# New durations for a planner's idle work and first loads, in the opening of a fused attention and expert kernel

## Chip, cores and metric

The kernel runs on one core of one Trainium2 chip. The metric is the device time in microseconds (us) of one execution; the median of eight runs before the change is 1723.44 us (1723.06 to 1723.79). Engines are named as in the profile: PE multiplies matrices, DVE, ACT and POOL work on tiles, SP issues most loads and stores.

## What is computed

Linear attention, normalised, is followed by a weighted sum over four two-layer experts. All of it is in fp32.

```python
# attention: 8 batches, 8 heads, 576 positions, head dimension 64
kv  = np.einsum('bhsd,bhse->bhde', k, v)
out = np.einsum('bhsd,bhde->bhse', q, kv)
rms = np.sqrt(np.mean(out * out, axis=-1, keepdims=True) + 1e-06)
x   = (out / rms * g_norm)            # then (B,H,S,D) -> (B*S, H*D): 4608 rows of 512
# experts: E = 4, D = 512, F = 1024
p = domain_probs / (domain_probs.sum(-1, keepdims=True) + 1e-09)
for e in range(E):
    h = np.maximum(x @ w1[e], 0.0)
    out += p[:, e:e + 1] * (h @ w2[e])
```

## The kernel before, in words

**Stages.** The 4608 rows form nine chunks of 512: one for each of the eight batches (its first 512 positions) and a ninth of the eight remainders of 64 positions. A stage is one chunk with one expert, so there are 36. Each stage has a product up (x by w1, then relu) and a product down (hidden by w2). The very first product up is plain (`up_plain`, L999: 16 groups of two 128x512 products). All others use recursive forms with seven products in place of eight, one or two levels deep (`up`, L912; `down`, L1126; `down_deep`, L1201), whose operand sums are adds on DVE or POOL (L360). Attention of batch c+1 is computed inside stage c.

**Attention of a batch** runs per pair of heads: q is turned by PE (L651) and copied by ACT (L656); k by v is summed on PE (L665) and copied (L678); the attention product follows (L691) into the PSUM banks db and u in batch 0, db or ab later; ACT squares (L564), DVE reduces (L571), POOL takes the power -1/2 (L578, L582), DVE multiplies (L591), PE turns the result (L709), and ACT copies it scaled by the gain (L717). The 64 remaining positions go the same way through L735, L753 and L769. In batch 0 this is done pair by pair, in the others two pairs at a time.

**Who decides the order.** Nothing is ordered by hand. Every operation is given to a planner (`Plan.add`) with a key, a cost in us for each engine that could run it, the buffers it touches and, for loads, a size. At build time `Plan.layout` plays all engines forward: at each moment an engine that is free takes, among operations whose inputs and buffers are ready by the planner's clock, the one with the earliest due time (PE and SP: the first in key order that is ready). An add that either DVE or POOL may do goes to whichever takes it first. Tile slots are given out in the same pass. What comes out is one fixed list for each engine; on the chip every engine works through its list in that order and waits on semaphores.

**Loads in the planner.** A load costs SP 0.55 us; its end is taken from a bus that starts at a fixed time and moves 215 KB a us (L169), with eight loads in flight at most (LANES, L171). The size that a load is given (`kb`) is used for that alone, not for the transfer itself. In the opening SP loads q, k and v of the four pairs of batch 0, then the four quarters of w1 of expert 0, then q, k and v of batch 1.

**Idle work.** While PE is in the opening (its next operation has a key under 0) and nothing is ready for it, the planner inserts idle operations (L204 to L217): two transposes of the identity (L1353) into a bank of ab or db that nobody uses. Each is planned at 0.23 us. They are part of PE's list for good: PE executes them whether or not the next operation could already start.

The lines that set this before the change:

```python
105        bus, port = 3.0, 0.0
169                        bus = max(bus, t + 1.5) + op.kb / 215.0
170                        op.end = bus + 0.5
204                if eng == "PE" and busy[eng] <= t and 1.6 <= t and front < idle_until:
209                        op = Op(front, {"PE": 0.23}, None, (), (), 0, False)
```

Of the kernel before, what the change touches and what calls it, by code (L numbers as in the profile page):

```python
# [16 lines left out]
class Buf:  # L17


    def __init__(self, kind, name, ap=None):  # L20
        self.kind, self.name, self.ap = kind, name, ap
        self.writers, self.readers, self.left, self.slot = [], [], 0, None
# [12 lines left out]
class Plan:  # L35
# [13 lines left out]

    SPARE = {"big": 6, "small": 3}  # L50
    STEP, LATE = 44.0, 20.0

    def __init__(self):
        self.ops = []
# [26 lines left out]
    def layout(self, slots, later, idle, idle_banks, idle_until):  # L81
# [20 lines left out]
                cross = self.SAME if op.cost.keys() == d.cost.keys() else self.CROSS  # L102
                d.due = min(d.due, op.due - cross - min(d.cost.values()))
        busy = {e: 0.0 for e in todo}
        bus, port = 3.0, 0.0
        lanes = [0.0] * self.LANES
        t = 0.0
        wake = [0.0, 1.6]
# [24 lines left out]
        while left:  # L133
            moved = False
            while todo["PE"] and todo["PE"][0].start is not None:
                todo["PE"].pop(0)
            front = todo["PE"][0].key if todo["PE"] else 1e9
            for eng in todo:
                if busy[eng] > t:
                    continue  # L140
                pending = todo[eng]
                while pending and pending[0].start is not None:
                    pending.pop(0)
                if not pending:
                    continue
                reach = pending[0].key + self.REACH[eng]
                best = None
                for op in pending:
                    if op.key > reach:
                        break  # L150
                    if op.start is not None:
                        continue
                    if best is not None and op.due >= best.due:
                        continue
                    when = ready(op, eng)
                    if when is None:
                        continue
                    if when > t:
                        heapq.heappush(wake, when)
                        continue  # L160
                    best = op
                    if eng in ("PE", "SP"):
                        break
                if best is not None:
                    op = best
                    op.start, op.eng = t, eng
                    if eng == "SP":
                        busy[eng] = t + op.cost[eng]
                        bus = max(bus, t + 1.5) + op.kb / 215.0  # L169
                        op.end = bus + 0.5  # L170
                        lanes = lanes[1:] + [op.end]  # L171
                    else:
                        op.end = busy[eng] = t + op.cost[eng]
                        if op.kb:
                            op.end += 9.0 if op.kb == 512 else 5.5
                    if op.port:
                        port = op.end
                        heapq.heappush(wake, port)
                    for b in op.outs:
                        if b.kind is not None and b.slot is None:  # L180
                            free[b.kind].sort()
                            b.slot = free[b.kind].pop(0)[1]
                            b.ap = slots[b.kind][b.slot]
                    for b in op.bufs:
                        b.left -= 1
                        if b.left == 0 and b.kind is not None:
                            end = max(o.end for o in [op] + b.readers + b.writers) + self.CROSS
                            free[b.kind].append((end, b.slot))
                            live[b.kind] -= 1
                            ended[b.kind] = max(end, ended.get(b.kind, 0.0))  # L190
                            for rule in [r for r in later if not any(live.get(k) for k in r[0])]:
                                later.remove(rule)
                                end = max(ended[k] for k in rule[0])
                                for ap in rule[2]:
                                    free.setdefault(rule[1], []).append((end, len(slots[rule[1]])))
                                    slots[rule[1]].append(ap)
                                heapq.heappush(wake, end)
                    heapq.heappush(wake, busy[eng])
                    heapq.heappush(wake, op.end + self.SAME)
                    heapq.heappush(wake, op.end + self.CROSS)  # L200
                    order.append(op)
                    left -= 1
                    moved = True
                if eng == "PE" and busy[eng] <= t and 1.6 <= t and front < idle_until:  # L204
                    kind, spare = next((
                        (k, f) for k in idle_banks for f in free[k] if f[0] <= t
                    ), (None, None))
                    if spare is not None:
                        op = Op(front, {"PE": 0.23}, None, (), (), 0, False)
                        op.start, op.eng, op.end = t, eng, t + 0.23  # L210
                        op.fn = lambda eng, bank=slots[kind][spare[1]]: idle(bank)
                        busy[eng] = op.end
                        free[kind].remove(spare)
                        free[kind].append((op.end, spare[1]))
                        heapq.heappush(wake, op.end)
                        order.append(op)
                        moved = True  # L217
            if moved:
                continue
            while wake and wake[0] <= t:  # L220
                heapq.heappop(wake)
            assert wake, ("no operation can start", t, left, {
                e: (todo[e][0].key, todo[e][0].fn) for e in todo if todo[e]
            }, {k: len(v) for k, v in free.items()})
            t = heapq.heappop(wake)
# [5 lines left out]
def kernel(  # L231
# [41 lines left out]
    NT = 512  # L273
    NR = NT // P
# [5 lines left out]
    KR = 6  # L280
# [83 lines left out]
    def load(key, buf, dst, src, kb, reads=(), also=()):  # L364
        plan.add(
            key, SPC, lambda eng: nc.sync.dma_start(out=dst(), in_=src), reads=reads,
            parts=[buf] + list(also), kb=kb,
        )
# [40 lines left out]
    def w1_src(e, dh, uh):  # L409
        rows = moe_w1[e][dh * 2 * P:(dh + 1) * 2 * P, uh * HF:(uh + 1) * HF]  # L410
        return rows.rearrange("(kt p) f -> p kt f", p=P)
# [19 lines left out]
    def weights_1(e, key, step, need):  # L431

        f = {n: Buf("big", f"w1_{e}_{n}") for n in (1, 2, 21, 4, 5, 6, 7, 3)}
        corner = {}
        w1corner[e] = {}
        for i, (n, dh, uh) in enumerate(((1, 0, 0), (2, 1, 0), (21, 0, 1), (4, 1, 1))):
            corner[n] = Buf(None, f"w1c_{e}_{n}")
            w1corner[e][uh, dh] = f[n], corner[n]
            load(
                key + i * step, f[n],  # L440
                lambda n=n: f[n].ap[:].rearrange("p (k u) -> p k u", k=2),
                w1_src(e, dh, uh), 512, also=[corner[n]],
            )

        def form(k_, o, a, b, op):
# [155 lines left out]
    def attention(b, key, span, rem):  # L601
# [9 lines left out]
        def load_pair(hp):  # L611
            hs = slice(2 * hp, 2 * hp + 2)
            n = f"{b}_{hp}"
            kind = "kv" if b or hp < 2 else "big"
            kt, vt, qt = Buf(kind, f"k{n}"), Buf(kind, f"v{n}"), Buf("small", f"q{n}")
            want = at(hp) - 0.25 if b else key - 1 + 0.1 * hp
            for r in range(2):
                load(
                    want, qt,
                    lambda qt=qt, r=r: qt.ap[:].rearrange(  # L620
                        "p (r h d) -> p r h d", h=2, d=D)[:, :, r, :],
                    q[b, 2 * hp + r, 0:NT, :].rearrange("(p r) d -> p r d", r=NR), 128,
                )
            for t, src in ((kt, k), (vt, v)):
                load(
                    want, t,
                    lambda t=t: t.ap[0:KP, 0:2 * KR * D].rearrange("p (h x) -> p h x", h=2),
                    src[b, hs].rearrange("h (p j) d -> p h (j d)", j=KR), 288,
                )
            return kt, vt, qt  # L630

# [4 lines left out]
        for g, pairs in enumerate(groups):  # L636
            n = f"{b}_{g}"
# [85 lines left out]
        n = f"{b}_r"  # L723
# [584 lines left out]
    plan.add(-2.85, {"SP": 1.1}, load_gains, writes=[gains], kb=1)  # L1308
    attention(0, -2.0, 1.3, 0.1)
    sums_1 = weights_1(0, -2.5, 0.02, 0.3)  # L1310
    up_plain(0, 0, 0, 0.0, 1.0)
    sums_1()
# [44 lines left out]
    with tc.manual_schedule(engines={ENG.PE, ENG.DVE, ENG.Activation, ENG.Pool, ENG.SP}):  # L1357
# [4 lines left out]
        for op in order:  # L1362
            if op.seed:
                bank, n = op.marks
# [39 lines left out]
```

## Time and profile before

| | |
|---|---|
| median of 8 runs | 1723.44 us (1723.06 to 1723.79) |
| the profiled execution | 1723.65 us, of which the span in the trace is 1721.9 us |
| instructions in the trace | 39248 |
| idle transposes in PE's built list | 114 |
| DMA moved | 230.42 MB, mean 134 GB/s |

How to read it: the span is the time from the first to the last recorded instruction, and all times in the trace count from its start. A timeline line gives start, length, engine, line, operation, output and inputs, shapes, and a count where equal instructions were merged; in brackets stands the idle time before it and what ended it. In fp32 a product is two matmul records in the trace, a transpose one. A matmul's recorded length includes its passage through the array, so the distance between the starts of two groups, and not the length, is what a group costs when PE is full. A line of waits gives who waited for whom, the total in us, how often, and the longest. A line of DMA issues ends with the median us from issue to landing.

### The profile page before, as it was taken

The numbers are of one execution on the slowest core, as the hardware profiler recorded it, in microseconds if no ns is written. First come the engines' busy times: TensorE is split into PE (matmuls) and PEld (weight loads), VectorE is DVE, ScalarE is ACT, GpSimd is POOL, SyncE is SP. The second block draws the span as 40 slices with busy tenths as digits, with TensorE's granted clock in tenths as the row PEclk, the third lists the DMA queues.
The fourth block names the chain that finished last, engine by engine and source line by source line (L and its number), as shares of the span: only waits on it lengthen the run. The fifth ranks groups of instructions, "written<-read, shape, count | busy, mean of one in ns | idle before, by whom it ended". The sixth has DMA issues, their size and how long they took to land.

```text
span 1721.9 us, 39248 instructions
## 1 busy us (share of the span) xinstructions
PE 1712.6 (99%) x15586; PEld 1653.8 (96%) x15586; DVE 1234.7 (72%) x2034; ACT 973.9 (57%) x2378; POOL 677.0 (39%) x613
## 2 busy tenths in 40 slices
PE   9999999999999999999999999999999999999998
PEld 7699999999999999999999999999999999999998
DVE  4755655565777777777778787777788787777774
ACT  3354544454455665565666566566666666656562
POOL 2421322133435443433355554433355554433331
PEclk9999999999999999999999999999999999999999
DMA  9756434633456354444478444444478444444442
GB/s 235 219 163 198 143 117 142 198 130 114 169 142 152 102 114 106 111 111 109 127 172 194 111 111 111 111 111 109 103 183 204 116 111 111 111 111 111 100 110 49
DMA packets 156567, 230.42 MB, mean 134 GB/s; under 512 B 49888, under 2 KB 97248, under 8 KB 156384
## 3 DMA queue, kind: packets, MB, share of 16 engines
q1 hardware_dynamic: 133312, 191.21, 36.0%
q0 software_dynamic: 23072, 36.71, 14.4%
q8 instruction: 122, 2.00, 0.5%
q14 instruction: 61, 0.50, 0.1%
HBM read 154.74 MB, written 73.14 MB: 132 GB/s over the span
## 4 chain that ended last, share of the span: by engine, by line
PE 99%; POOL 0%; DVE 0%; ACT 0%; issue 0%; POOLq 0%
PE u L912 45%; PE db L1201 21%; PE ab L1201 13%; PE db L1126 12%; PE u L999 2%; PE ab L665 1%; PE ab L709 1%; PE ab L1353 1%; PE ab L651 1%; PE ab L691 1%; PE u L1126 1%; PE ab L1126 0%; PE db L691 0%; POOL rt L582 0%; PE ab L753 0%; PE ab L735 0%
## 5 line engine op out<-in xcount | busy, mean ns | idle before, releaser
L360 DVE TENSOR_TENSOR big<-big,big 128x1024 f32<-128x1024 f32 (+1 forms) x446 | 439.7, 1000 | 30.6 <-ACT big L895 19.4
L912 PE MATMUL u<-xf,big 128*128 128x128 f32 x3104 | 452.4, 275 | 0.0
L912 PEld LDWEIGHTS u<-xf,big 128*128 128x128 f32 x3104 | 399.8, 192 | 1.4
L912 PE MATMUL u<-xf,w1y 128*128 128x128 f32 x2652 | 390.9, 275 | 0.0
L939 DVE TENSOR_TENSOR big<-u,snap 128x256 f32<-128x256 f32 x442 | 186.5, 422 | 232.4 <-PE u L912 162.1
L912 PEld LDWEIGHTS u<-xf,w1y 128*128 128x128 f32 x2652 | 343.2, 192 | 1.6
L931 ACT ACTIVATE snap<-u 128x256 f32<-128x256 f32 x490 | 187.8, 383 | 207.5 <-PE u L912 175.5
L931 ACT ACTIVATE big<-u 128x256 f32<-128x256 f32 x442 | 169.2, 383 | 120.7 <-PE u L912 93.3
L360 POOL TENSOR_TENSOR big<-big,big 128x256 f32<-128x256 f32 (+1 forms) x137 | 180.5, 1321 | 127.2 <-DVE big L360 61.4
L1126 PE MATMUL db<-big,big 128*128 128x256 f32 x904 | 214.4, 380 | 2.1 <-DVE big L591 2.1
L1126 PEld LDWEIGHTS db<-big,big 128*128 128x128 f32 x904 | 163.5, 191 | 19.9 <-DVE big L591 2.3
L1201 PE MATMUL db<-big,big 128*128 128x128 f32 x1204 | 166.8, 275 | 0.0
L1201 PEld LDWEIGHTS db<-big,big 128*128 128x128 f32 x1204 | 150.4, 192 | 0.1
L895 ACT ACTIVATE big<-big 128x1024 f32<-128x1024 f32 x128 | 134.6, 1051 | 4.0 <-DVE big L360 3.3
L1229 ACT ACTIVATE snap<-db 128x256 f32<-128x256 f32 x216 | 76.8, 356 | 105.7 <-PE db L1201 102.8
L1096 POOL DMA_DIRECT2D out_dram<-big x98 | 89.7, 1042 | 56.3 <-ACT big L1073 37.9
L360 POOL TENSOR_TENSOR big<-big 128x512 f32<-128x512 f32 (+1 forms) x56 | 67.6, 1208 | 108.8 <-DVE big L360 58.5
L1201 PE MATMUL ab<-kv,big 128*128 128x128 f32 x764 | 110.1, 275 | 0.0
L1201 PE MATMUL db<-kv,big 128*128 128x128 f32 x752 | 109.1, 275 | 0.0
L931 ACT ACTIVATE u<-u 128x256 f32<-128x256 f32 x245 | 90.8, 370 | 32.4 <-PE u L912 12.4
L1267 POOL TENSOR_TENSOR big<-big 128x512 f32<-128x512 f32 x25 | 31.7, 1269 | 177.6 <-DVE big L360 144.4
L578 POOL TENSOR_SCALAR ss<-ss 128x16 f32<-128x16 f32 (+2 forms) x26 | 6.4, 245 | 241.6 <-DVE ss L571 241.4
(218 smaller groups left out, 2925.7 us busy)
## 6 DMA issues: line engine op xcount, KB each, us to landing
xf<-x SPq DMA_DIRECT2D x108, 512.0 KB, 3.7
out_dram<-big POOLq DMA_DIRECT2D x82, 256.0 KB, 5.7
xf<-x_h SPq DMA_DIRECT2D x81, 256.0 KB, 3.2
xf<-x SPq DMA_DIRECT2D x81, 256.0 KB, 3.4
x<-xf SPq DMA_DIRECT2D x36, 512.0 KB, 6.2
big<-in_moe_w_dram SPq DMA_DIRECT2D x29, 512.0 KB, 5.8
small<-in_q_dram SPq DMA_DIRECT2D x72, 128.0 KB, 4.8
kv<-in_k_dram SPq DMA_DIRECT2D x30, 288.0 KB, 5.1
```

Source lines behind the costliest of these rows:

```text
L360: lambda eng: adder(eng).tensor_tensor(out=out_(), in0=a(), in1=b(), op=op),
L651: nc.tensor.transpose(bank.ap[:, rs], qt.ap[:, rs], ident[:])
L895: lambda eng: nc.scalar.activation(out=b.ap[:], in_=b.ap[:], func=ACT.Relu),
L912: nc.tensor.matmul(ps.ap[:, u * P:(u + 1) * P], lhsT=w1f[e][m][mm][1]()[:, u * P:(u + 1) * P], rhs=views[m][mm][1](), start=(mm in (1, 5) ...
L931: lambda eng: nc.scalar.activation(out=where(), in_=ps.ap[:, 0:HN], func=ACT.Copy),
L939: lambda eng: nc.vector.tensor_tensor(out=block(whole, a, t), in0=src.ap[:, 0:HN], in1=add_.ap[:], op=ALU.add),
L999: nc.tensor.matmul(bank.ap[:], lhsT=two(w.ap[:])[:, kt, ut * P:(ut + 1) * P], rhs=two(xh[dh].ap[:])[:, kt, :], start=(dh == kt == 0), stop ...
L1096: nc.gpsimd.dma_start(out=dst, in_=cell(i)[parts, :], accum_op=ALU.add)
L1126: nc.tensor.matmul(ps.ap[:, 0:HN], lhsT=four(h[m])[:, kt // 2, t, kt % 2, :], rhs=w2f[e][m].ap[:, kt * HN:(kt + 1) * HN], start=(m in (1, ...
L1201: nc.tensor.matmul(ps.ap[:, o * P:(o + 1) * P], lhsT=b.ap[:, col:col + P], rhs=w2q[e][m][mm][1]()[:, kt, :], start=(mm in (1, 5) and o == ...
L1229: lambda eng: nc.scalar.activation(out=where(), in_=group_of(ps.ap), func=ACT.Copy),
L1267: lambda eng: adder(eng).tensor_tensor(out=whole(to), in0=whole(a), in1=whole(b), op=ALU.add),
```

## The change

Four numbers that the planner reads at build time are replaced. Two transposes of idle work are planned at 0.43 us while the planner's clock is under 6.8 us, and at 0.23 us after that. The bus starts at 3.8 us instead of 3.0. The loads of batch 0 and of the first weights are given other sizes for the bus: a half of q 157 instead of 128, k and v 241 instead of 288 each, a quarter of w1 of expert 0 312 instead of 512. Everything later keeps its numbers. The transfers themselves, the arithmetic and the tiles are the same; the lists that the planner writes for the engines are new. Lines after the two added ones move down by one or two, so that L651 is L653 in the new kernel, L999 is L1001, and so on.

```diff
     STEP, LATE = 44.0, 20.0
+    SLOW = 6.8
...
-        bus, port = 3.0, 0.0
+        bus, port = 3.8, 0.0
...
-                        op = Op(front, {"PE": 0.23}, None, (), (), 0, False)
-                        op.start, op.eng, op.end = t, eng, t + 0.23
+                        took = 0.43 if t < self.SLOW else 0.23
+                        op = Op(front, {"PE": took}, None, (), (), 0, False)
+                        op.start, op.eng, op.end = t, eng, t + took
...
-                w1_src(e, dh, uh), 512, also=[corner[n]],
+                w1_src(e, dh, uh), 512 if e else 312, also=[corner[n]],
...
-                    q[b, 2 * hp + r, 0:NT, :].rearrange("(p r) d -> p r d", r=NR), 128,
+                    q[b, 2 * hp + r, 0:NT, :].rearrange("(p r) d -> p r d", r=NR), 128 if b else 157,
...
-                    src[b, hs].rearrange("h (p j) d -> p h (j d)", j=KR), 288,
+                    src[b, hs].rearrange("h (p j) d -> p h (j d)", j=KR), 288 if b else 241,
```

## The prediction

> **What bounds the kernel now.** I read the page's table of engines first, then PE's list of waits, then PE's timeline of the opening, then the windows around the one long wait, then the landing times of single loads.
>
> ```profile
> PE 1712.6 (99%) x15586; PEld 1653.8 (96%) x15586; DVE 1234.7 (72%) x2034; ACT 973.9 (57%) x2378; POOL 677.0 (39%) x613
> PE 99%; POOL 0%; DVE 0%; ACT 0%; issue 0%; POOLq 0%
> ```
>
> PE is busy 99% of the span and is 99% of the chain that ended last, so the time is the sum of what PE executes, useful or idle, plus its few waits. PE's list of waits up to 80 us is complete in five lines; from 80 us to the end the same list is empty.
>
> ```profile
> PE db L1126 <- DVE big L591: 2.1, 1, 2.1
> PE ab L1353 <- POOL ident masks.py:199: 1.3, 1, 1.3
> PE u L912 <- ACT snap L931: 0.6, 1, 0.6
> PE u L912 <- ACT u L931: 0.5, 1, 0.5
> PE ab L709 <- ACT big L717: 0.2, 1, 0.2
> ```
>
> The columns are total us, count and longest. 1.3 us is the start. The other four stand between 67 and 78 us and are the only late waits of the run: 0.52 + 0.57 + 2.09 + 0.16 = 3.34 us by the timeline. There is none in the opening, because idle transposes (L1353) fill it:
>
> ```profile
> 1.35 5.91 PE L1353 MATMUL ab<-ident 128*128 128x128 f32 x30 [1.35 <-POOL ident masks.py:199]
> 7.10 0.60 PE L651 MATMUL ab<-ident,small 128*128 128x128 f32 x4
> 7.53 2.35 PE L1353 MATMUL ab<-ident 128*128 128x128 f32 x20
> 9.81 0.92 PE L665 MATMUL ab<-kv,kv 96*64 96x64 f32 x24
> ...
> 28.11 1.91 PE L1353 MATMUL ab<-ident 128*128 128x128 f32 x16
> ```
>
> Columns: start, length, instruction. The first 30 take 5.91 us, 0.197 us each; the next 20 run from 7.53 to 9.81, 0.114 each; 16 from 28.11 to 29.86, 0.109 each; blocks of 12 (12.31 to 13.77) 0.122 each. I use 0.116 as the mean price of one at full pace. The wait of 2.09 us costs more than itself:
>
> ```profile
> 71.47:74.89 3.42, 1.55 (x7) 1.33 (x8) 2.06 (x5) 0.00 (x0) 3.25 (x4) 0.96 0.37 90
> 74.89:78.30 3.41, 3.25 (x16) 2.43 (x15) 0.91 (x3) 1.72 (x4) 1.49 (x3) 0.54 0.47 155
> ```
>
> ```profile
> 73.34 2.58 PE L1126 MATMUL db<-big,big 128*128 128x256 f32 x8 [2.09 <-DVE big L591]
> 75.71 1.06 PE L709 MATMUL ab<-ident,big 128*128 128x128 f32 x4
> ```
>
> In the windows the first pair of numbers is length and PE's busy time; the granted clock is third from the end. PE was busy only 1.55 of 3.42 us, and for the next 3.41 us the clock was 0.54. Eight L1126 took 73.34 to 75.71 = 2.37 us where elsewhere they take 1.73 (78.25 to 79.98), four L709 0.99 where elsewhere 0.44. Half a pace over 3.41 us is 1.7 us lost. So the profiled execution, 1723.65 us (span 1721.9 and 1.75 around it; 0.2 above the median 1723.44), holds 3.34 + 1.7 = 5.0 us of late loss.
>
> **The change, part by part.** No arithmetic, tile or load size changes; only numbers that the planner reads. So its effect is the order of the built program, which I compare with the old one engine by engine.
>
> *Idle work.* The built program has 92 idle transposes for 114: 22 fewer. Their places: before the first L651 (now L653) 22 for 30, then 12 for 20, and later blocks of 6 to 8 before the k/v products for 2 and 12; the block before the last L711 of the batch is 10 for 16. The clock is at half pace until about 6.6 us by time (26.8 transposes at 0.197 from 1.35), whatever is executed, so each one left out is worth the full pace: 22 x 0.116 = 2.55 us, if nothing else is late. Adding the differences up block by block, and setting the results beside the landings (issue plus time to landing of the single load): first k/v product 9.81 - 16 x 0.116 = 7.95, v lands at 2.79 + 4.7 = 7.5; second 13.77 - 18 x 0.116 = 11.7, v at 5.21 + 5.7 = 10.9; third 17.73 - 20 x 0.116 = 15.4, v at 8.89 + 5.7 = 14.6; fourth 21.47 - 2.3 = 19.15, v at 12.19 + 6.3 = 18.5. Each has 0.5 us or more in hand. The fourth L711 ends at 30.30 - 2.55 = 27.75.
>
> *Batch 1 is pulled forward, into loads that are not there yet.* In the old order four products of L999 are done before the next L651 at 33.73; in the new one two, and the L651 (now L653) for batch 1 follows the fourth L711 at once, at 27.75. SP's order is the same up to these loads, and each issue waits for a landing eight loads earlier, so I leave their landings where they are. The three that now matter:
>
> ```profile
> small<-in_q_dram SPq DMA_DIRECT2D x1, 128.0 KB, 11.9
> small<-in_q_dram SPq DMA_DIRECT2D x1, 128.0 KB, 10.7
> kv<-in_v_dram SPq DMA_DIRECT2D x1, 288.0 KB, 7.3
> ```
>
> The last column is us from issue to landing; the issues are at 16.52, 20.77 and 27.88. So q of the first pair lands at 28.4: wait 0.65. L653 (0.44) and one product (1.72) later the q of batch 0's remainder is wanted at 30.6 and lands at 31.5: wait 0.85 after the small overheads. L737, a product, L653 and L755 (0.39, 1.8, 0.44, 0.6) end at 34.8; the v of batch 1's second pair lands at 35.2: wait 0.4. Sum 1.9 us. Bounds: nothing (SP issues earlier because tiles come free about 2 us earlier) to 1.9 and a half-paced stretch of 1.7. I take 1.9 without it: the wait that lowered the clock left PE idle 1.87 of 3.42 us, 0.57 us in 3.41 (68.06 to 71.47) did not, and the largest here is 0.85. The opening then nets 2.55 - 1.9 = 0.65 us.
>
> *The late waits.* The old 2.09 us wait is the bank db: attention's results of the second half of batch 1 (L691, done at 63.54) lay in it until DVE's L591, which waited for POOL's power. POOL first ran a 128x1024 add (66.02, 2.35 us) and the power then took 68.45 to 72.57. Chain: squares 1.1, reduction 1.2, POOL's add 2.4, power 4.1, first half of L591 0.75; with the gaps 9.8 us, to 73.34. In the new order no 128x1024 add stands ahead of that power on POOL; six small ones do (0.45, 0.73 or 1.2 us each, 4.0 together), and they end before the reduction. Chain without it: 1.1 + 1.2 + 3.2 to 4.1 + 0.75 = 6.3 to 7.2 us (the first half of batch 2 in the old trace: POOL starts at 89.48, its power ends at 92.67, so 3.2). Between the two PE now has four products (6.9), L755 (0.6), one group of L914 (0.45) and 0.2 of changeovers: 8.2 us. So at least 1.0 in hand, and the wait goes. The next L914 groups no longer follow each other: a group of L1128 (1.73), L711 and L771 stand between the first and second write of bank u, where the seed copy (0.37) was late by 0.52; for the later snapshot copy about 1.0 us is in hand. What is late next is the second L1128, whose operand comes from a 128x1024 add on POOL: by the same sum done at 68.4 to 69.2, wanted at 71.0. I take all four waits and the half pace as gone: 5.0 us, bounded by nothing and 5.0.
>
> *Work moved between engines.* DVE loses 42 instructions (2036 to 1994), POOL gains them: 35 adds of 128x128, 0.28 us on DVE and 0.45 on POOL, and 15 of 128x512 (0.68 and 1.21), against a few larger ones back. That is some 20 us more on POOL, which is idle 1045 us. What hides it is PE's own 99%; if that cover failed once, the price is one wait like the old one, 2.09 + 1.7 = 3.8. Nothing or 3.8: I take nothing, since the old order has no PE wait in the 1640 us after 80. PE's order after about 700 us is the same list in lines and shapes, the last stretch included.
>
> Sum on the profiled execution: 1723.65 - 2.55 + 1.9 - 3.34 - 1.7 = 1718.0 us. Against the median it is 1717.8; I keep 1718.0.
>
> The Trainium skill, "TensorE: Matmul & The Clock Gate", section "Part 1: The HAM clock gate", speaks against the new constant: it says that the clock's window runs freely, so that the slow stretch at a kernel's start differs from run to run and should not be fitted. This trace shows one edge, near 6.6 us. By the page the edge could lie 3.4 us earlier; then my first product would meet v's landing, and the loads would return most of it, 1718 plus or minus half a microsecond as an estimate. The same section says that the clock falls back after an idle window of about 3.4 us. The row above differs: 1.87 us idle of 3.42 was enough. By the page new load waits would never cost 1.7 more; by the row a wait near 2 us does.
>
> **Rivals.** (1) *A load wait lowers the clock.* For it: three waits within 8 us, on loads that take 7 to 12 us to land. Against: none is near 1.87 us. Time 1718.0 + 1.7 = 1719.7. (2) *A wait takes the place of the old one* at the first L1128: if the chain is the old 9.8 us instead of 7.2, PE waits 9.8 - 8.2 = 1.6 and the clock falls for 1.7: 1721.3. For it: POOL's power ran 2.9 to 3.76 us for one shape, and DVE now carries eight small adds between the two reductions and L593. Against: the POOL queue as listed. (3) *Slower: POOL becomes late in the attention of batches 2 to 7.* Place: from a remainder's L755 to its L771 the new order leaves 6.2 to 6.6 us of PE work, the old 7.0, while POOL has 35 more small adds in its queue ahead of such powers. The chain there is 0.65 + 0.7 + 1.9 to 3.2 + 0.75 = 4.0 to 5.3. It decides from 6.6: each us beyond costs one us in each of 6 batches, and from 8.1 the 9 us lost outweigh the gain; with a 128x1024 add ahead (2.35) it reaches 7.7, so 1718.0 + 6 x 1.1 and two half-paced stretches of 1.7 give 1728. (4) *The change does not act*: excluded, the built order differs from PE's first block on.
>
> **How the numbers follow.** Forecast, waits gone or nearly (1716.4 to 1719.5): 0.55. Rival 1: 0.12. Rival 2 (1720 to 1722.6): 0.18. Rival 3: 0.10. Something smaller between 1722.6 and 1727: 0.05. The range 1716.4 to 1722.6 reaches from load waits of 0.3 to rival 2 and leaves out 0.15 to 0.2. 0.2% is 3.4 us, about what a measurement of this kernel can tell from no change: below 1720.0 is faster (0.55 and most of rival 1, 0.65), above 1726.9 slower (0.10), the rest 0.25.
>
> **What the new profile would show.** Idle transposes 22 and 12 around the first L653, and the first L667 near 8 us; PE waits on DMA of q and v between 27 and 36 us, 1.9 in sum; no PE wait on DVE L593 and a granted clock of 1.0 between 60 and 80; no PE wait after 80. Wrong would be a clock under 1.0 after 7 us, or PE waits on POOL or DVE in the attention of batches 2 to 7.

## The result, and the profile after

Both kernels ran on the same chip:

| kernel | median us | lowest to highest | runs | ratio to before, 95% interval |
|---|---|---|---|---|
| before | 1723.45 | 1722.63 to 1723.79 | 28 | |
| changed | 1717.56 | 1716.68 to 1720.03 | 10 | 0.9968 [0.996, 0.9976] |

The change gained 5.9 us; the forecast was 1718.0 us, from 1716.4 to 1722.6. The profiled execution took 1716.98 us, of which the span is 1715.2. Its page, table of engines (busy time, share, instructions) and the chain that ended last:

```profile
PE 1708.3 (100%) x15564; PEld 1650.2 (96%) x15564; DVE 1239.2 (72%) x1992; ACT 973.9 (57%) x2378; POOL 691.8 (40%) x655
PE 99%; DMA 0%; SPq 0%; DVE 0%; issue 0%
```

TensorE executes 4.3 us less than the 1712.6 before. Its whole list of waits is now three lines (total us, count, longest):

```profile
PE ab L1355 <- POOL ident masks.py:199: 1.4, 1, 1.4
PE ab L653 <- DMA small<-in_q_dram: 0.5, 1, 0.5
PE ab L667 <- DMA kv<-in_v_dram: 0.4, 1, 0.4
```

The four late waits are gone. The two new ones are on loads, but at the first q and the first v of batch 0, not on batch 1's loads. TensorE's timeline of the opening (start, length, instruction) shows where:

```profile
1.35 4.27 PE L1355 MATMUL ab<-ident 128*128 128x128 f32 x22 [1.35 <-POOL ident masks.py:199]
6.09 0.63 PE L653 MATMUL ab<-ident,small 128*128 128x128 f32 x4 [0.47 <-DMA small<-in_q_dram]
6.56 1.47 PE L1355 MATMUL ab<-ident 128*128 128x128 f32 x12
8.46 0.92 PE L667 MATMUL ab<-kv,kv 96*64 96x64 f32 x24 [0.42 <-DMA kv<-in_v_dram]
...
22.94 3.60 PE L1001 MATMUL u<-big,big 128*128 128x512 f32 x8
26.37 0.60 PE L711 MATMUL ab<-ident,big 128*128 128x128 f32 x4
26.81 1.26 PE L1355 MATMUL ab<-ident 128*128 128x128 f32 x10
27.90 0.60 PE L711 MATMUL ab<-ident,big 128*128 128x128 f32 x4
28.34 0.38 PE L653 MATMUL ab<-ident,small 128*128 128x128 f32 x2
```

The blocks of 22 and 12 are where they were forecast. The first L667 came at 8.46 instead of 7.95, the first L653 of batch 1 at 28.34 without a wait. The late stretch, in the same view:

```profile
55.19 1.16 PE L693 MATMUL db<-kvbd,small 64*64 64x64 f32 x64
56.28 1.98 PE L1001 MATMUL u<-big,big 128*128 128x512 f32 x4
58.20 0.68 PE L755 MATMUL ab<-kvbd,small 64*64 64x64 f32 x16
58.81 5.42 PE L1001 MATMUL u<-big,big 128*128 128x512 f32 x12
64.06 0.61 PE L914 MATMUL u<-big,big 128*128 128x128 f32 x4
64.51 1.89 PE L1128 MATMUL db<-big,big 128*128 128x256 f32 x8
```

Between L693, which fills bank db, and the first L1128, which needs it back, stand the four products, L755 and one group of L914. L1128 starts without a wait; in the kernel before it waited until 73.34. In the windows (length and TensorE's busy time first, granted clock third from the end) nothing is lost where 0.54 stood:

```profile
71.47:74.89 3.42, 3.42 (x66) 2.99 (x68) 3.02 (x7) 1.69 (x4) 0.33 (x2) 1.00 0.67 173
74.89:78.30 3.41, 3.41 (x78) 3.14 (x79) 3.00 (x8) 1.36 (x3) 1.60 (x3) 1.00 1.06 281
```

### The profile page after: what moved, and what is told of

The parts are those of the page before. It is cut to its first block, busy times and chain, and to the rows that moved or that the text cites. A ratio compares the mean times of both kernels' runs of the same rounds, so it can differ in the third digit from the quotient of the medians.

```text
span 1715.2 us, 39187 instructions
## 1 busy us (share of the span) xinstructions
PE 1708.3 (100%) x15564; PEld 1650.2 (96%) x15564; DVE 1239.2 (72%) x1992; ACT 973.9 (57%) x2378; POOL 691.8 (40%) x655
## 4 chain that ended last, share of the span: by engine, by line
PE 99%; DMA 0%; SPq 0%; DVE 0%; issue 0%
PE u L914 45%; PE db L1203 21%; PE ab L1203 13%; PE db L1128 12%; PE u L1001 2%; PE ab L667 1%; PE ab L711 1%; PE ab L653 1%; PE ab L693 1%; PE u L1128 1%; PE ab L1355 0%; PE ab L1128 0%; DMA kv<-in_v_dram 0%; PE ab L755 0%; PE db L693 0%; PE ab L737 0%
## 5 line engine op out<-in xcount | busy, mean ns | idle before, releaser
L914 PE MATMUL u<-xf,big 128*128 128x128 f32 x2816 | 412.4, 275 | 0.0
L914 PE MATMUL u<-xf,w1y 128*128 128x128 f32 x2652 | 391.1, 275 | 0.0
L914 PEld LDWEIGHTS u<-xf,big 128*128 128x128 f32 x2816 | 364.3, 192 | 2.0
L941 DVE TENSOR_TENSOR big<-u,snap 128x256 f32<-128x256 f32 x436 | 184.0, 422 | 239.9 <-PE u L914 155.8
L914 PEld LDWEIGHTS u<-xf,w1y 128*128 128x128 f32 x2652 | 343.7, 192 | 1.7
L1128 PE MATMUL db<-big,big 128*128 128x256 f32 x920 | 217.0, 380 | 0.0
L1128 PEld LDWEIGHTS db<-big,big 128*128 128x128 f32 x920 | 166.7, 190 | 18.6
L1203 PE MATMUL db<-big,big 128*128 128x128 f32 x1304 | 178.1, 275 | 0.0
L1203 PEld LDWEIGHTS db<-big,big 128*128 128x128 f32 x1304 | 161.7, 192 | 0.1
L362 POOL TENSOR_TENSOR big<-big 128x512 f32<-128x512 f32 (+1 forms) x67 | 82.3, 1231 | 120.0 <-DVE big L362 61.6
L914 PE MATMUL u<-xf,small 128*128 128x128 f32 x720 | 108.3, 275 | 0.0
L1203 PE MATMUL ab<-kv,big 128*128 128x128 f32 x740 | 106.0, 275 | 0.0
L1203 PE MATMUL db<-kv,big 128*128 128x128 f32 x720 | 103.3, 275 | 0.0
```

Of the source, the lines that this page charges most:

```text
L362: lambda eng: adder(eng).tensor_tensor(out=out_(), in0=a(), in1=b(), op=op),
L914: nc.tensor.matmul(ps.ap[:, u * P:(u + 1) * P], lhsT=w1f[e][m][mm][1]()[:, u * P:(u + 1) * P], rhs=views[m][mm][1](), start=(mm in (1, 5) ...
L941: lambda eng: nc.vector.tensor_tensor(out=block(whole, a, t), in0=src.ap[:, 0:HN], in1=add_.ap[:], op=ALU.add),
L1128: nc.tensor.matmul(ps.ap[:, 0:HN], lhsT=four(h[m])[:, kt // 2, t, kt % 2, :], rhs=w2f[e][m].ap[:, kt * HN:(kt + 1) * HN], start=(m in (1, ...
L1203: nc.tensor.matmul(ps.ap[:, o * P:(o + 1) * P], lhsT=b.ap[:, col:col + P], rhs=w2q[e][m][mm][1]()[:, kt, :], start=(mm in (1, 5) and o == ...
```

## The experiments

Theory: nearly all of the gain is the late stretch (3.34 us of waits and 1.7 us of lower clock), and the opening nets well under 1 us, since loads take back what idle work gives. Rival: the shorter opening is the gain. All kernels compute the whole reference. The kernel before had medians of 1723.35, 1723.63 and 1723.42 us in the three sets below.

**Set 1: the parts of the change, and the late wait by itself.**

*e1_idle_only* has the new pace of idle work, and the old start of the bus and load sizes. Against the changed kernel:

```diff
-        bus, port = 3.8, 0.0
+        bus, port = 3.0, 0.0
-                w1_src(e, dh, uh), 512 if e else 312, also=[corner[n]],
+                w1_src(e, dh, uh), 512, also=[corner[n]],
```
(and 128 and 288 for all of q, k and v)

> The change's idle durations alone: SLOW and 0.43 stay, the bus (3.0) and the sizes of the loads (128, 288, 512) are those of before. The built list has 92 idle transposes, as in the changed kernel, but the old order around the late wait: one product, L755 and seven groups of L914 between the second L693 of batch 1 and the first L1128, and a 128x1024 add on POOL ahead of that half's power. Two-part theory (22 idle transposes 2.55 us less some 0.5 to 1.9 of load waits, and separately 5.0 us of late waits and half-paced clock that the new order removes): the late part stays, 1723.45 - 2.55 + 0.5 to 1.9 = 1721.4 to 1722.8. Rival (the whole gain is the shorter opening, the late waits go because everything starts earlier): 1718 to 1719.

Measured 1723.42 (1722.72 to 1724.6, 11 runs), ratio 1.0002 [0.9993, 1.001]: **no gain at all**, a miss. It has 92 idle transposes like the changed kernel, in other blocks (16 and 12 around the first L653). L755 starts at 63.26 for 65.45 in before, 2.2 us earlier. But the waits between 60 and 80 us grew from 3.34 to 4.5 us (in this list of the whole run 0.4 of those on ACT snap stand after 80 us):

```profile
PE u L914 <- DVE big L941: 1.4, 1, 1.4
PE db L1128 <- DVE big L593: 1.4, 1, 1.4
PE ab L1355 <- POOL ident masks.py:199: 1.4, 1, 1.4
PE u L914 <- ACT u L933: 0.9, 1, 0.9
PE u L914 <- ACT snap L933: 0.9, 3, 0.5
PE ab L711 <- ACT big L719: 0.4, 1, 0.4
```

```profile
64.65:68.06 3.41, 2.32 (x16) 1.94 (x16) 3.41 (x6) 1.74 (x6) 3.02 (x3) 1.00 1.08 312
68.06:71.47 3.41, 1.42 (x8) 1.04 (x8) 2.23 (x6) 0.54 (x2) 3.41 (x1) 1.00 0.98 396
71.47:74.89 3.42, 2.48 (x6) 2.03 (x7) 2.37 (x5) 0.00 (x0) 1.98 (x3) 0.59 0.96 271
```

In the windows the second pair of columns after TensorE's is VectorE's, then ScalarE's, then GpSimd's: DVE is busy 3.41 of 3.41 us and then POOL 3.41 of 3.41, while TensorE has 1.42. The order there is not the old one, which had been expected. On TensorE's timeline of before, and below it of e1:

```profile
62.45 1.16 PE L691 MATMUL db<-kvbd,small 64*64 64x64 f32 x64
63.54 1.98 PE L999 MATMUL u<-big,big 128*128 128x512 f32 x4
65.45 0.68 PE L753 MATMUL ab<-kvbd,small 64*64 64x64 f32 x16
```

```profile
62.28 1.16 PE L693 MATMUL db<-kvbd,small 64*64 64x64 f32 x64
63.26 0.65 PE L755 MATMUL ab<-kvbd,small 64*64 64x64 f32 x16
```

The product behind L691 stands ahead of L693 in e1. So the chain through DVE and POOL, which begins with L693, starts only 0.2 us earlier, and no longer has that product over it. Of the 2.2 us the first L1128 keeps 0.9 (72.41 for 73.34), and the clock still falls to 0.59. After 80 us the two waits on ACT snap take 0.4; where the rest goes was not traced. As the order is another, e1 does not price the shorter opening by itself.

*e2_loads_only* is the opposite part: the changed kernel with the old pace.

```diff
-                        took = 0.43 if t < self.SLOW else 0.23
+                        took = 0.23
```

> The new sizes and the later bus alone; idle work planned at 0.23 us throughout. The built list has 120 idle transposes (40 before the first L653), 6 more than before, and in the late stretch three products, L755 and five groups of L914 between the second L693 of batch 1 and the first L1128, with no 128x1024 add on POOL directly ahead of that half's power. Two-part theory: the opening costs 6 x 0.116 = 0.7 us more than before, the late 5.0 us are gone or nearly: 1723.45 + 0.7 - 5.0 = 1719.1 (1718.6 to 1720.6). Rival (the gain is the shorter opening): 1724.1.

Measured 1719.26 (1718.56 to 1720.37, 9 runs), ratio 0.9977 [0.9968, 0.9987]: as expected. With *more* idle work than before (120 for 114) it keeps 4.1 of the 5.9 us. One late wait is left, 0.6 us on ACT u.

*e3_power_first* takes the kernel before and removes only the cause that was named for the late wait: the 128x1024 add of POOL ahead of the second-half power runs on DVE, and the two adds that read its result stand behind the scaling.

```diff
+    for op, other in ((chain[2], scale[1]), (chain[1], scale[0]), (chain[0], before_six)):
...
+        order.remove(op)
+        order.insert(order.index(other) + 1, op)
+    chain[0].eng = "DVE"
```

> The kernel before, its opening untouched with 114 idle transposes; only the 128x1024 add that stood on POOL ahead of the power of batch 1's second half runs on DVE instead, and the two adds that read it come behind the scaling (L591) on DVE. Two-part theory: POOL takes the power 2.4 us earlier, PE's wait of 2.09 us on L591 and the half-paced 3.4 us after it go, three waits of 0.5, 0.6 and 0.2 stay: 1723.45 - 2.09 - 1.7 = 1719.7 (1719.2 to 1720.7), clock 1.0 between 70 and 80 us. Rival (the late waits are tied to the opening): 1723.4. Third case (the wait goes, the clock falls all the same): 1721.4.

Measured 1720.97 (1719.81 to 1721.36, 11 runs), ratio 0.9985 [0.9976, 0.9994]. The 2.09 us wait is gone and the clock is 1.0 between 58 and 81 us, so the cause is shown; but 2.4 us were gained, not 3.7. Its list has 0.4 us on DVE and 0.4 on ACT at L709 in place of 0.2, and the first idle block took 6.42 us for 5.91: together 1.1 of the missing 1.3.

*e4_idle_restored* gives the changed kernel its 22 idle transposes back, without a change to the rest of the order.

```diff
+    for fill, more in ((fills[-1], 3), (fills[1], 4), (fills[0], 4)):
+        n = fill[0][-1]
+        order[n:n] = [order[n]] * more
```

> The changed kernel's order on every engine, with 22 idle transposes put back: 8 in the first block (30), 8 in the second (20), 6 in the last of the batch (16), so 114 as before. Two-part theory: they cost 22 x 0.116 = 2.55 us less the load waits that they cover (0.9 us in the profiled execution): 1717.56 + 1.7 = 1719.2 (1718.6 to 1720.1); the runs spread less (1.2 us as before, against 3.4), because the idle work again covers loads that land at different times. Rival (the loads bind the opening, idle work costs nothing): 1717.6.

Measured 1718.88 (1718.18 to 1720.54, 10 runs), ratio 0.9975 [0.9966, 0.9984]. The time was as expected; the spread did not shrink as expected (2.4 us). By the medians 22 idle transposes are worth 1.3 us, half of the 2.55 forecast (0.8 against the changed kernel's repeat e10, below); the intervals of the ratios overlap, so this is not clear of noise.

**Set 2: which number does it, and what idle work is worth.**

*e6_w1_size_only* is the kernel before with one number changed; *e7_all_but_w1* the changed kernel with that number put back:

```diff
-                w1_src(e, dh, uh), 512, also=[corner[n]],
+                w1_src(e, dh, uh), 512 if e else 312, also=[corner[n]],
```

> The kernel before with only the size of the first w1 loads changed from 512 to 312. The opening is instruction for instruction that of before (114 idle transposes); from there on the list puts the second-half power of batch 1 behind no 128x1024 add on POOL. Theory (the late stretch is the gain, the w1 size is the number that moves it): the late waits of 3.3 us go but for 0.5 to 0.6 on ACT, and the 1.7 us of half-paced clock: 1718.8, within 1718.2 to 1720. Rival (the late waits go only when the opening's times fit, so the bus and the sizes of q, k and v are needed): 1722.5 or more.

> The changed kernel with the w1 loads' size put back to 512. The opening is that of the changed kernel, 92 idle transposes, and the late stretch is another order: twelve products of u directly behind the last transposes of batch 1 and then those of the down part, with small POOL work but no 128x1024 add ahead of the second-half power. Theory (what counts is the w1 size): the late stretch is too short for the chain of batch 1 through DVE and POOL, waits of 3 to 5 us in 60 to 75 us, 1721.5 within 1720.5 to 1723.5. Rival (the bus, the sizes of q, k, v and the pace of the idle work are enough): 1717 to 1719.

| median us | w1 at 512 | w1 of the first expert at 312 |
|---|---|---|
| other numbers as before (114 idle) | 1723.63 | 1718.53, e6, ratio 0.9972 [0.996, 0.9983] |
| other numbers as changed (92 idle) | 1723.93, e7, ratio 1.0001 [0.9992, 1.001] | 1717.56 (e10 below: 1718.08) |

Both went the theory's way (e7 0.4 us above its range). **The w1 size alone is worth 5.1 us, all the rest nothing without it and 0.5 to 1.0 us with it,** the last no more than these kernels spread. The size moves no byte; the planner believes that w1 is there sooner, and takes batch 1's attention earlier among the products. In e6 L691 stands at 59.98 and the first L1126 at 70.22, 10.2 us apart and with no wait on the scaling. In e7 the second L693 comes at 63.28, only L755 and groups of L914 follow it, and its list of waits opens, behind the start, with

```profile
PE db L1128 <- DVE big L593: 1.2, 1, 1.2
PE u L914 <- DVE big L941: 1.2, 1, 1.2
PE u L914 <- ACT snap L933: 0.9, 3, 0.5
```

There no 128x1024 add stands ahead of the power on POOL, and the wait is there all the same: the products over the chain count, not the add alone. From the end of that L691 (L693) to the first L1126 (L1128) TensorE's own work, waits taken off, is 4.9 us in e7, 5.1 in e1 and 6.6 in before, which wait; it is 8.2 in the changed kernel and 8.6 in e6, which do not.

*e8_idle_and_power* is e1 with the add moved as in e3.

> The kernel of the idle pace alone (1723.4), with the 128x1024 add that POOL runs ahead of the second-half power of batch 1 put on DVE, and the DVE add that reads it behind the scaling that the power feeds. Theory (the 22 idle transposes saved shift the real work forward, and the late chain through POOL's power takes it back): with the chain freed the saving shows, 1719.6, within 1718.6 to 1721, and no wait over 1 us on L593. Rival (DVE itself, busy all of 64.65 to 68.06 us there, holds the late stretch): 1722 or more, with the wait on DVE's L941 and L593 still there.

Measured 1720.17 (1719.61 to 1720.68, 11 runs), ratio 0.998 [0.9971, 0.9989]; no wait on L593 over 0.4 us, clock 1.0. The theory's number, so DVE alone does not hold this stretch; 0.6 us on DVE's L941 and 1.4 on ACT stay. With the chain freed, the idle cut that gave nothing in e1 gives 0.8 us against e3's 1720.97, in another set and with overlapping intervals.

*e5_no_idle* is the changed kernel without any idle transpose:

```diff
+    order = [o for o in order if o.bufs or "PE" not in o.cost]
```

> The changed kernel without any idle transpose: the 92 that are left in the opening (and any later) are taken out, the order of all real work stays. Theory A (idle work only fills time in which TensorE would wait for loads anyway; the clock also rises under the real work, which between the pairs covers 2.4 of every 3.5 us): 1717.5 within 1716.5 to 1719.5, the first product of the experts within 0.5 us of the 22.94 of the changed kernel, waits on loads in the list in place of the idle work. Theory B (idle work holds the clock up): the granted clock stays at a half through the opening, the real work of four pairs, about 9.4 us at full pace, runs at about 0.55 of it and ends about 7 us later, less the about 4.5 us that the idle work between the pairs leaves free: 1720 to 1726. I expect A's end of it or a little more, 1719, within 1717.5 to 1721.

Measured 1716.76 (1715.54 to 1717.74, 5 runs), ratio 0.996 [0.9948, 0.9973]: below what I expected and in theory A's range. In the opening load waits take the place of 92 transposes. Theory B shows in part: the first two L667 take 1.55 us for 0.92, and the clock falls to 0.56 from 20.52 to 23.94 us; the kernel is no slower for it.

**Set 3: the margin, the spread, the best version.**

*e9_power_twice* runs the power of the second half of batch 1 twice on POOL, in the changed kernel.

```diff
+    def twice(eng, once=power.fn, ss=power.outs[0], rt=power.outs[1]):
+        once(eng)
+        nc.gpsimd.tensor_tensor(
+            out=rt.ap[0:P, 0:16], in0=ss.ap[0:P, 0:16], in1=mhalf[0:P, 0:16], op=ALU.pow)
```

> The changed kernel with the second-half power of batch 1 (POOL, 128x16, at 59.89, 3.16 us) run twice, the second time with the same operands into the same tile. In the changed kernel the scaling on L593 that waits for it runs 63.08 to 64.33 and the first product of L1128 starts at 64.51: the cover left over is 0.2 us. Theory (the chain of last transposes of batch 1, squares, power and scaling is just covered by the products that the new order puts over it): 2.9 to 3.2 us more on POOL give a wait of about 2.9 on L593 before the first L1128, 1720.5 within 1719.8 to 1722.5, the upper half if the clock falls too. Rival (the new order has room to spare there and the gain came from elsewhere): within 0.5 us of the changed kernel, 1717 to 1718.2.

Measured 1720.35 (1719.19 to 1723.35, 11 runs), ratio 0.9985 [0.9976, 0.9993]. The second power took 2.90 us and the old wait is back, on TensorE's timeline and in the windows:

```profile
64.97 0.61 PE L914 MATMUL u<-big,big 128*128 128x128 f32 x4
67.81 1.97 PE L1128 MATMUL db<-big,big 128*128 128x256 f32 x8 [2.23 <-DVE big L593]
```

```profile
64.65:68.06 3.41, 1.19 (x7) 0.78 (x6) 1.09 (x2) 0.94 (x3) 3.24 (x3) 1.00 0.93 316
68.06:71.47 3.41, 3.41 (x24) 2.90 (x24) 2.71 (x4) 1.66 (x5) 3.41 (x3) 1.00 0.04 9
```

A wait of 2.23 us from 2.90 us more: 0.7 us was in hand. (I had read 0.2, by the end of the second scaling; L1128 starts 0.84 us after the first one begins, at 66.97, and needs only that half.) The clock stayed at 1.00 behind it in this execution. Of the eleven, five list a mean clock of 1.000 for the run and took 1719.19 to 1720.35 us, this one among them; six list 0.999 and took 1719.88 to 1723.35. The old half-paced stretch is 0.001 of a run, so it may have come back in some of them; this column is too coarse to tell.

*e10_after_again* is the changed kernel once more, *e12_no_idle_again* e5 once more beside it, and *e11_late_idle_only* keeps 28 of the 92 idle transposes:

```diff
+    drop = {n for f in fills[:5] + fills[11:] for n in f[0]}
+    order = [o for n, o in enumerate(order) if n not in drop]
```

> The changed kernel once more, for its spread, a second profile and a comparison beside the two that follow: 1717.6 within 1716.9 to 1718.3. If the load waits that were forecast at 27 to 36 us come and go with the moment at which loads land, this profile may show them (up to 1.9 us) or waits of 0.4 to 0.5 at the first q or v or at the last v, as in the runs so far; in either case the waits on loads sum to 0 to 2 us.

> The changed kernel with 28 of its 92 idle transposes: those of the third and fourth pair of batch 0 (15 to 23 us); the five blocks before and the last block of 10 are gone. Without any idle work the four real steps from 19.6 to 26.9 us ran at a lower pace (1.16 for 0.92, 1.12 for 0.60, 4.04 for 3.60 us), about 1.2 us in sum, of which the later waits hide a part. Theory (only loads and the clock at the end of the opening count): 1716.4, within 1715.8 to 1717.2, the fastest of all. Rival (the early idle work holds the clock for the later steps): 1717.3 or more.

> The changed kernel without any idle transpose once more, beside the changed kernel on one chip: 1716.8, within 1716.2 to 1717.4. If the 92 idle transposes are worth nothing, this is 0.3 to 1.2 us below the changed kernel; if they are worth something, it is at or above it.

| kernel | idle transposes | median us | lowest to highest | ratio to before |
|---|---|---|---|---|
| e10, changed | 92 | 1718.08 | 1717.06 to 1718.63 | 0.9968 [0.9956, 0.998] |
| e11 | 28 | 1717.38 | 1716.74 to 1717.79 | 0.9964 [0.9951, 0.9976] |
| e12 | 0 | 1717.05 | 1716.32 to 1717.4 | 0.9961 [0.9949, 0.9974] |

e10's time and e12's are as expected; e11, expected fastest, is not, and lies 0.1 us inside its rival's range, which its spread of 1.0 us does not decide (its profile holds a lone wait of 1.6 us on ACT snap between 1200 and 1500 us). e12 is 1.0 us under the changed kernel and e5 0.8, but the ranges overlap and it is under what this measurement can tell: the 92 idle transposes, some 13 us of TensorE, are worth about nothing. The lists of e10 and, below it, e12:

```profile
PE ab L1355 <- POOL ident masks.py:199: 1.4, 1, 1.4
PE ab L667 <- DMA big<-in_v_dram: 1.3, 1, 1.3
PE ab L653 <- DMA small<-in_q_dram: 0.5, 1, 0.5
PE ab L667 <- DMA kv<-in_v_dram: 0.3, 1, 0.3
```

```profile
PE ab L653 <- DMA small<-in_q_dram: 6.7, 2, 5.3
PE ab L667 <- DMA big<-in_v_dram: 1.5, 2, 1.1
PE ab L667 <- DMA kv<-in_v_dram: 1.5, 1, 1.5
PE ab L737 <- DMA small<-in_q_dram: 0.9, 1, 0.9
PE ab L711 <- DVE big L593: 0.3, 1, 0.3
```

e12's load waits sum to 10.6 us: loads set the opening's pace, and most of the idle work only stands in them.

## Why the prediction was right

- **The late stretch, 5.0 us, was right in its cause, and in size to about 1 us.** e6 gains 5.1 with the old opening, though waits of 0.6 on ACT u and 0.4 on ACT kvbd stay in its profile. e3, e8 and e9 take the chain's wait away or put it back, with 2.4, 3.3 and about 2.5 us. "At least 1.0 in hand" was 0.7 (e9): the reduction, the mean on POOL (0.73 us) and the power (3.16) ended 0.3 to 0.5 us later than summed. Rival 2 was that close.
- **"22 x 0.116 = 2.55 us, if nothing else is late": the price holds, the condition did not.** In the four profiles with this opening (changed, e10, e9, e7) the last L711 of batch 0 starts at 27.90, 28.77, 27.67 and 28.17 us, for 29.86 in before: 1.1 to 2.2 us earlier. Up to there they wait 0.89, 1.98, 0.72 and 1.23 us on loads; 2.55 less that falls 0.3 to 0.5 short of what they gained, and the earlier edge of the clock (below) has the right sign for the rest. In whole times it shows as 0.8 to 1.3 us (e4) and 0.8 (e3 to e8), and as nothing in e1. "Each has 0.5 us or more in hand" failed: q0 and v0 landed later than TensorE came in the changed kernel's own profile.
- **"1.9 us in sum" of load waits at 27 to 36 us: the place failed, the size was near.** In four profiles of the same opening the load waits sum to 0.89 (changed), 1.98 (e10), 1.54 (e9) and 1.23 us (e7), mean 1.4, mostly on q and v of batch 0. Only e9 shows one of the three named waits, 0.82 us at L737 where 0.85 was forecast. The same q landed in the changed kernel just as L737 ran. Which load is late differs between executions; I had taken one trace's landings as fixed; that the sum came near on other loads is luck.
- **The opening's net, 0.65 us, fits the times but is not measured by itself.** Beside 5.0 us the medians leave 0.9 (5.9) and 0.3 (e10). e6 to the changed kernel is 1.0 (e10: 0.45), but e6 keeps its two late waits. By the profiles, at the last L711 and less e9's 0.82 behind it, it is more: 1.1 to 2.0 us.
- **"The clock is at half pace until about 6.6 us by time, whatever is executed" was wrong twice.** The 0.197 us it rests on is a mean over both paces. Windows of 0.6 us with TensorE's count in brackets show 4 or 5 transposes at the low pace and 8 at the full one. The edge of the changed kernel, and below it that of e6:

```profile
3.75:4.35 0.60, 0.60 (x4) 1.00 0.72 178
4.35:4.95 0.60, 0.60 (x6) 1.00 0.97 326
4.95:5.55 0.60, 0.60 (x7) 1.00 1.12 319
```

```profile
6.15:6.75 0.60, 0.60 (x5) 1.00 1.14 192
6.75:7.35 0.60, 0.60 (x4) 1.00 1.03 220
7.35:7.95 0.60, 0.60 (x8) 1.00 1.07 275
```

Read so, it lies near 4.6 us in the changed kernel, 4.3 to 4.7 in e4, e7, e9 and e10, 5.4 in e2, 6.3 in before, 6.9 in e1 and 7.3 in e3 and e6. The opening's list does not fix it: e1 and e8 have the same one, and four L653 that start at 5.04 us in both take 0.88 us in e1 and 0.46 in e8. And without idle work it comes with the real work: e5 runs its first two L667, at 7.90 and 11.49, in 1.55 us and the third, at 15.16, in 0.92. The Trainium skill, "TensorE: Matmul & The Clock Gate", section "Part 1: The HAM clock gate", which calls the window free-running and the edge not to be fitted, agrees with these rows in that the edge moves; the half microsecond that it gives for the movement is too little here. What the new constant fits is an edge that moves by 3 us.
- **Rivals.** (1) did not act: e10's 1.25 us wait is followed by 0.92 for L667 and 0.60 for L711, the full pace; without idle work it did, in e5. (3) did not act: no wait after 80 us in the changed kernel, and POOL's "some 20 us more" were 14.8 (677.0 to 691.8). By rival 3's own sum the forecast gain of 5.4 is used up at 7.5 (6.6 + 5.4 / 6), not at 8.1. (4) is out by the profile.
- **Cause of the spread.** The changed kernel spreads over 3.35 us, before over 1.16. Landings that differ by about 1 us and the clock's edge are both seen; e4, with the idle work back, still spreads over 2.4, so idle work is not what steadies it. What part each has stays open.

## What to carry to other kernels

A planner's constant acts only through the order it makes: change the numbers one at a time, and look for the one wait that moves (here a load size that moves no byte, worth 5.1 of 5.9 us). Filler cut from a bound engine is worth only what the next bound leaves, here loads first and a DVE and POOL chain later, so price it by the next landing and by the cover of the longest chain behind it, not by its own length. Doubling the suspected instruction measures the margin of a cover directly.

## What the runs showed of the hardware

- The length of a wait does not alone decide the clock. 2.22 us idle of 3.41 left it at 1.00 in e9's profile, 1.87 us of 3.42 behind two shorter waits was followed by 0.54 in the kernel before, 1.99 of 3.41 behind 1.09 by 0.59 in e1, and 1.74 of 3.42 behind 0.77, on loads, by 0.56 in e5. The page named above speaks of a fall after an idle window of about 3.4 us; no window of the kernel before was idle so long, and all three falls came after less. Where the chip's own window lies on these stretches is not in the trace.
- The granted clock's column does not show the slow start: it reads 1.00 from 3.43 to 6.86 us in e5, where four L653 take 1.08 us for 0.60.
- The same 128x16 power on POOL took 2.90, 3.16, 3.19 and 3.76 us in these profiles, and the 128x16 mean ahead of it 0.20 to 1.32. The mean over a run's 14 powers is 3.41 us before and 2.96 in the changed kernel; why was not traced.
